# Where the block's closing barrier stands: behind the last projections or ahead of them

## The chip, the cores and the metric

The kernel runs on one core of one Trainium2 chip. The metric is the device time of one execution in microseconds (us), the slowest core's, which here is the only one. A profiled execution also has a *span*: the time from its first to its last recorded instruction. The device time is longer than the span by a time that no trace covers; that remainder is called "time minus span". All runs told of here are marked fast in the record.

In the profile's lines PE is TensorE, which multiplies matrices, DVE is VectorE, ACT ScalarE, POOL GpSimd and SP SyncE. The trace also records the clock that PE was granted: it is full (1.00) or half (0.50; in the trace of before 68 records of each), and it changes only on a grid of 3.413 us. A stretch between two points of this grid is called a *clock window* below, and how the grid lies against the kernel differs from execution to execution (it has a point at 1309.09 us in the profile of before). "Landing" is the moment when the data of a load has arrived.

## The reference, cut to what matters

Two one-token attention blocks whose results are concatenated. A has 32 heads over 32768 cached keys each, B has 32 query heads on 8 cached heads and looks at the last 4096 keys.

```python
def _A_ref(x, k_cache, v_cache, wq, wo):            # x 1x1x512, caches 1x32x32768x128, bf16
    q = (x @ wq).reshape(B, Sq, H, Dh).transpose(0, 2, 1, 3)
    scores = einsum("bhqd,bhkd->bhqk", q, k_cache) * Dh ** -0.5
    o = einsum("bhqk,bhkd->bhqd", softmax(scores), v_cache)
    return o.transpose(0, 2, 1, 3).reshape(B, Sq, H * Dh) @ wo     # wo 4096x512
# B: the same on k_cache[:, :, -4096:], each cached head repeated for 4 query heads
# result: concatenate([a, b], axis=-1), 1x1x1024
```

The caches that have to be read make 570 MB, so the kernel streams them and hides everything else behind the stream. Only its last 12 us concern us: the last head of A is finished (the products with V, called PV, and then the *gather*, two matmuls that collect the heads' results), spread over the partitions (the *spread*), and multiplied with `wo`; the row of B is multiplied with its `wo` there too.

## The kernel before

Every operation is recorded with its engine and its dependencies, and then each engine's list is emitted inside one block. At the end of the block all engines meet in a barrier. Behind it SyncE waits for the two stores of the output.

```python
def build(self):
    ...
    with nc.Block() as block:
        block.gpsimd(self.emit("pool"))
        block.vector(self.emit("dve"))
        block.scalar(self.emit("act"))
        block.sync(self.emit("sp"))
        block.tensor(self.emit("pe"))
    for n in self.X:                       # behind the closing barrier
        nc.sync.wait_ge(self.outsem[n], 16)

def emit(self, eng):
    ...                                    # what precedes the loop, the loop over the heads,
    def body(e):                           # and what follows it (post)
        ...
        with e.Fori(0, nit):
            ...
            for name, sem in sems.items():             # ends every pass of the loop: semaphores are set back
                e.sem_inc(sem, -step[name])._wait_ge(sem, step[name])
        ...
        straight(e, post, seen, base)

def plan(self):
    ...
    self.loop = {}
    for n in ("B", "A"):
        for part in range(len(self.WO_CUTS[n]) - 1):
            self.load_wo(n, part)          # wo of B in 2 pieces, wo of A in 6, each with its semaphore
    self.emit_spread("A")
    self.emit_proj()

def emit_spread(self, name):
    ...
    ri = self.op("dve", ... reciprocal(rinv, row sum) ..., self.gath)
    ob = self.op("dve", ... tensor_scalar_mul(ob, numerators, rinv) ..., ri)
    o = self.op("pe", mm, ob, self.k_sel)              # 4 matmuls: psT <- ob, spread
    t["ozop"] = self.op("dve", ... tensor_copy(oz, p2) ..., o)
```

`emit_proj` then has PE multiply B (32 matmuls into `psS`), lets VectorE copy the result to `pb`, sums it over the partitions (`psACC`), and multiplies A with the six pieces of its `wo` as they land (`psT`, then `psPT`). VectorE and ScalarE copy the two halves of the row to `out_sb`, and SyncE stores it.

Of the kernel before, what the change touches and what calls it, by code (L numbers as in the profile page):

```python
# [35 lines left out]
class Op:  # L36
# [2 lines left out]



    __slots__ = ("eng", "fn", "deps", "loop", "pos", "to", "users", "before", "alts")

    def __init__(self, eng, fn, deps, to, loop, alts=None):
        self.alts = alts
        self.eng = eng
        self.fn = fn
        self.deps = [d for d in deps if d is not None]
        self.to = to
        self.loop = loop  # L50
        self.users = []


class _Kernel:
# [31 lines left out]


    def op(self, eng, fn, *deps, to=None, alts=None):
        o = Op(eng, fn, deps, to, self.loop.get(eng), alts)
        self.prog[eng].append(o)  # L90
        return o

    def build(self):
        nc = self.nc
        self.alloc()
        self.plan()
        self.early(2)
        self.sems = {}
        for e in self.engines:
            self.assign(e)  # L100
        with nc.Block() as block:
            block.gpsimd(self.emit("pool"))
            block.vector(self.emit("dve"))
            block.scalar(self.emit("act"))
            block.sync(self.emit("sp"))
            block.tensor(self.emit("pe"))
        for n in self.X:
            nc.sync.wait_ge(self.outsem[n], 16)

# [63 lines left out]
        return need  # L173

    def emit(self, eng):
        ops = self.prog[eng]
        nit = len({o.loop for o in ops} - {None})
        its = [[o for o in ops if o.loop == k] for k in range(nit)]
        first = next((i for i, o in enumerate(ops) if o.loop is not None), len(ops))
        pre, post = ops[:first], ops[first + sum(map(len, its)):]  # L180

        def run(e, o, waits, fn=None):
            for sem, val in waits:
                e.wait_ge(sem, val)
            inst = (fn or o.fn)(e)
            if o.to:
                inst.then_inc(self.sem(eng, o.to), 1)

        def straight(e, part, seen, base):
            for o in part:  # L190
                waits = []
                for name, (sem, val) in self.needs(o).items():
                    if val > seen.get(name, 0):
                        seen[name] = val
                        waits.append((sem, val - base.get(name, 0)))
                run(e, o, waits)

        def body(e):
            seen, base = {}, {}
            straight(e, pre, seen, base)  # L200
            if not nit:
                return

            assert len(set(map(len, its))) == 1
            need = [[self.needs(o) for o in it] for it in its]
            top = lambda k, name: max(n[name][1] for n in need[k] if name in n)
            sems = {name: sem for it in need[-2:] for n in it for name, (sem, _) in n.items()}
            step = {name: top(-1, name) - top(-2, name) for name in sems}
            for name in [x for x in sems if not step[x]]:
                if top(0, name) > seen.get(name, 0):  # L210
                    e.wait_ge(sems[name], top(0, name))
                    seen[name] = top(0, name)
                del sems[name]
            start = {name: top(-2, name) - step[name] * (nit - 1) for name in sems}
            plans = []
            for k, it in enumerate(need):
                cur, plan = {}, []
                for n in it:
                    w = []
                    for name, (sem, val) in n.items():  # L220
                        if name not in sems:
                            continue
                        rel = val - start[name] - step[name] * k
                        if rel > cur.get(name, 0):
                            cur[name] = rel
                            w.append((name, rel))
                    plan.append(sorted(w))
                plans.append(plan)
            for k, plan in enumerate(plans):
                for p, q in zip(plan, plans[-1]):  # L230
                    assert p == q or (k == 0 and set(p) <= set(q)), (eng, k, p, q)
            for name, sem in sems.items():
                if start[name] > 0:
                    e.sem_inc(sem, -start[name])._wait_ge(sem, start[name])
                elif start[name] < 0:
                    e.sem_inc(sem, -start[name])
            groups = []
            for o, w in zip(its[-1], plans[-1]):
                if not (groups and groups[-1][0] and o.alts):
                    groups.append((bool(o.alts), []))  # L240
                groups[-1][1].append((o, [(sems[name], rel) for name, rel in w]))
            odd = None
            if any(two for two, _ in groups):
                assert nit % 2 == 0
                odd = e.alloc_register(f"{eng}_odd")
                e.reg_mov(odd, 0)
            with e.Fori(0, nit):
                for two, part in groups:
                    if two:
                        with e.If_eq(odd, 0):  # L250
                            for o, w in part:
                                run(e, o, w, o.alts[0])
                        with e.Else():
                            for o, w in part:
                                run(e, o, w, o.alts[1])
                    else:
                        for o, w in part:
                            run(e, o, w)
                if odd is not None:
                    e.reg_sub(odd, 1, odd)  # L260
                for name, sem in sems.items():
                    e.sem_inc(sem, -step[name])._wait_ge(sem, step[name])
            for name in sems:
                base[name] = seen[name] = start[name] + step[name] * nit
            straight(e, post, seen, base)

        return body
# [126 lines left out]
    def plan(self):  # L394
        self.lsem = {"k": self.ksem, "v": self.vsem}
        self.fill = {w: [0, 0] for w in "kv"}
        self.free = {"k": [None] * 3, "v": [None] * 2}
        self.nbatch = 0
        self.copies = []
        self.pending = []  # L400
        self.psread = self.ptread = self.sread = self.accread = None
        self.gath = self.qcopy = self.hcopy = self.qread = None
        self.constants()
        a, b = self.X["A"], self.X["B"]

        self.load_wq("B")
        self.load_b("k", 0)
        self.load_wq("A")
        self.load_b("k", 1)
        self.emit_qproj("B")  # L410
        self.emit_unit("B", 0)
        self.emit_qproj("A")
        self.emit_stats("B", 0)
        self.emit_unit("B", 1, {1: lambda: self.emit_PT("B", 0)})
        self.emit_stats("B", 1)
        for g in range(2):
            if g == 1:
                self.emit_PT("B", g)
            self.load_b("v", g)
            self.emit_PV("B", g)  # L420
        self.emit_spread("B")

        for g in range(NQH):
            self.loop = {"pe": g, "dve": g // 2}
            self.load_k(g, 1 if 0 < g < NQH - 1 else 2)
            self.load_v(g)
            self.emit_qcopy(g)
            self.emit_unit("A", g)
            self.emit_stats("A", g)
            self.emit_PT("A", g)  # L430
            self.emit_PV("A", g)
        self.loop = {}
        for n in ("B", "A"):
            for part in range(len(self.WO_CUTS[n]) - 1):
                self.load_wo(n, part)
        self.emit_spread("A")
        self.emit_proj()

# [344 lines left out]
```

## Time and profile before

| | before |
|---|---|
| device time | 1322.43 us, median of 6 runs (1322.35 to 1322.94) |
| the profiled execution | span 1321.7 us, device time 1323.36 us |
| DMA | busy 9 tenths in 39 of 40 slices, 432 GB/s |
| last V rows landed | 1299.2 us |
| last piece of `wo` of A landed | 1318.8 us |

The cache stream bounds the kernel as far as 1299 us. From there PE and VectorE work in turns, with `wo` still arriving. The timeline of before, its PE and VectorE lines from the last gather to the summing of B (start, duration, engine, line, operation; in brackets the idle time before it and what ended it):

```profile
1308.19 0.41 PE L683 MATMUL psG<-oc_A,hw 128*32 128x128 f32 x2 [1.64 <-DVE oc_A L672]
1308.63 0.15 DVE L693 RECIPROCAL rinv_A<-psG 32x1 f32<-32x1 f32 x1 [0.50 <-PE psG L683]
1308.82 0.34 DVE L694 TENSOR_SCALAR ob_A<-psG,rinv_A 32x128 bf16<-32x128 f32 x1
...
1309.40 0.28 PE L698 MATMUL psT<-ob_A,spread 32*128 32x32 bf16 x4 [0.81 <-DVE ob_A L694]
...
1309.61 3.31 PE L733 MATMUL psS<-kbuf,oz_B 128*1 128x512 bf16 x32
...
1312.97 0.69 DVE L736 COPY pb<-psS 128x512 f32<-128x512 f32 x1 [3.07 <-PE psS L733]
...
1313.71 1.02 PE L737 MATMUL psACC<-pb,e 128*1 128x512 f32 x2 [0.80 <-DVE pb L736]
```

VectorE starts its reciprocal after the end of the gather (L683; 1308.59), and has done both of its steps at 1309.16. PE could not have gone on earlier: its sequencer, whose records are branches and semaphore instructions, is ending the last pass of the loop until 1309.34. The two run side by side.

The pages of the profile leave out semaphore instructions, but the trace has them. These are its records of the end of before (start, duration, engine, what it waits for and signals; S97 and S96 are the barrier's, S113 and S114 the two stores'):

```
1320.545  0.248  Sync    DMA_DIRECT2D     out_dram<-out_sb
1320.851  0.206  Sync    DRAIN            $S[97]== $S[96]++
1321.082  0.017  GpSimd  EVENT_SEMAPHORE  $S[96]>= $S[96]-=
1321.161  0.017  GpSimd  EVENT_SEMAPHORE  $S[97]+=
1321.202  0.017  Sync    EVENT_SEMAPHORE  $S[97]>= $S[97]--
1321.286  0.373  Sync    EVENT_SEMAPHORE  $S[114]>= $S[113]>=
```

The store's completion reached S113 at 1321.636. So the barrier took place while the store was under way, and SyncE still had 0.37 us to wait.

### The profile page before, as it was taken

The page shows a single profiled execution, that of the slowest core. Times are in us where ns is not written, and L with a number is a line of the kernel's source. Part 1 is how long each engine was busy: PE and PEld are TensorE (multiplying, and loading weights), DVE is VectorE, ACT ScalarE, POOL GpSimd, SP SyncE. Part 2 cuts the span into 40 slices and gives each one's busy share as a digit, 9 for nine tenths or more (in the row PEclk, how much of TensorE's full clock was granted, in tenths as well). Part 3 has the DMA queues.
Part 4 walks back from the last instruction along what each step waited for, and adds up shares of the span by engine and source line. Part 5 has one row for each costly group of instructions (what it writes and reads, how often), then busy time and mean ns, then how long its engine had stood idle before and what let it go on. Part 6 is the DMA issues. An engine that isn't in the chain of part 4 may idle for free. (4 is left out here: it accounts for less than half of the span.)

```text
span 1321.7 us, 28783 instructions
## 1 busy us (share of the span) xinstructions
PE 968.2 (73%) x13243; PEld 673.7 (51%) x13243; DVE 750.7 (57%) x1341; ACT 55.1 (4%) x168; POOL 2.6 (0%) x22
## 2 busy tenths in 40 slices
PE   4675768777677878767787777678777667877787
PEld 3353446555444655544465544446554445555453
DVE  3563556664555666455566645556665456665563
ACT  0000000000000000000000000000000000000000
POOL 0000000000000000000000000000000000000000
PEclk9886788887878888787888878888887788888788
DMA  9999999999999999999999999999999999999998
GB/s 404 434 434 431 440 434 434 434 436 432 433 436 436 428 438 434 428 438 434 428 442 430 428 442 432 430 438 434 437 432 432 438 430 434 438 428 436 436 428 365
DMA packets 13359, 570.59 MB, mean 432 GB/s; under 512 B 1570, under 2 KB 1700, under 8 KB 2084
## 3 DMA queue, kind: packets, MB, share of 16 engines
q1 hardware_dynamic: 13060, 570.43, 99.8%
q8 instruction: 8, 0.13, 0.0%
q10 hardware_dynamic: 288, 0.00, 0.0%
q14 instruction: 3, 0.02, 0.0%
HBM read 570.43 MB, written 0.00 MB: 432 GB/s over the span
## 5 line engine op out<-in xcount | busy, mean ns | idle before, releaser
L557 DVE COPY kt<-psT 128x1024 bf16<-128x1024 bf16 x1056 | 654.3, 683 | 236.9 <-PE psT L553 235.5
L553 PE MATMUL psT<-ident,kbuf 128*128 128x128 bf16 x8448 | 577.8, 234 | 169.0 <-DMA kbuf<-in_A_k_cache_dram 154.4
L553 PEld LDWEIGHTS psT<-ident,kbuf 128*128 128x128 bf16 x8448 | 538.1, 106 | 261.2 <-DMA kbuf<-in_A_k_cache_dram 162.5
L656 PE MATMUL psACC<-vbuf,ptsb 128*4 128x512 bf16 (+1 forms) x2112 | 187.0, 531 | 22.8 <-ACT ptsb L631 22.0
L576 PE MATMUL psS<-kt,qw 128*32 128x512 bf16 x2048 | 157.7, 385 | 14.9 <-DVE kt L557 14.9
L670 DVE TENSOR_SCALAR oc_A<-psACC,hot_A 128x128 f32<-128x128 f32 x32 | 11.2, 350 | 251.9 <-PE psG L683 251.9
L656 PEld LDWEIGHTS psACC<-vbuf,ptsb 128*4 128x4 bf16 (+1 forms) x2112 | 59.8, 111 | 140.4 <-issue 93.1
L604 ACT ACTIVATE psb<-psS,nb_A 128x512 bf16<-128x512 f32 x32 | 22.0, 687 | 1166.5 <-DVE nb_A L603 1166.5
L576 PEld LDWEIGHTS psS<-kt,qw 128*32 128x32 bf16 x2048 | 34.0, 95 | 57.6 <-DVE kt L557 30.8
L683 PE MATMUL psG<-oc_A,hw 128*32 128x128 f32 (+1 forms) x128 | 19.3, 227 | 52.3 <-DVE oc_A L672 52.3
L683 PEld LDWEIGHTS psG<-oc_A,hw 128*32 128x32 f32 x128 | 11.4, 109 | 62.4 <-DVE oc_A L672 55.0
L628 PE MATMUL psPT<-ident,psb 128*128 128x128 bf16 x136 | 18.3, 279 | 34.0 <-ACT psb L604 34.0
L672 DVE SCALAR_TENSOR_TENSOR oc_A<-psACC,hot_A,oc_A 128x128 f32<-128x128 f32 x96 | 33.6, 350 | 3.4
L593 DVE TENSOR_REDUCE tr_in<-psS 128x1 f32<-128x512 f32 x34 | 23.5, 692 | 17.2 <-PE psS L576 17.2
L628 PEld LDWEIGHTS psPT<-ident,psb 128*128 128x128 bf16 x136 | 10.3, 119 | 37.1 <-ACT psb L604 36.7
L597 PE MATMUL psACC<-rows,tr_in 128*1 128x64 f32 x64 | 8.7, 217 | 25.6 <-DVE tr_in L593 25.6
L631 ACT ACTIVATE ptsb<-psPT 128x512 bf16<-128x512 bf16 x34 | 20.3, 597 | 30.9 <-PE psPT L628 30.9
L597 PEld LDWEIGHTS psACC<-rows,tr_in 128*1 128x1 f32 x64 | 2.7, 81 | 35.1 <-DVE tr_in L593 35.1
L601 PE MATMUL psACC<-mr_A,nscale 1*128 1x1 f32 x64 | 12.1, 256 | 9.8 <-DVE mr_A L600 9.8
L601 PEld LDWEIGHTS psACC<-mr_A,nscale 1*128 1x128 f32 x64 | 9.4, 182 | 15.8 <-DVE mr_A L600 15.8
L603 DVE COPY nb_A<-psACC 128x1 f32<-128x1 f32 x32 | 5.0, 157 | 15.1 <-PE psACC L601 15.1
L600 DVE TENSOR_REDUCE mr_A<-psACC 1x1 f32<-1x64 f32 x32 | 6.8, 213 | 11.7 <-PE psACC L597 11.7
(82 smaller groups left out, 74.9 us busy)
## 6 DMA issues: line engine op xcount, KB each, us to landing
kbuf<-in_A_k_cache_dram SPq DMA_DIRECT2D x4, 4096.0 KB, 23.2
kbuf<-in_B_k_cache_dram SPq DMA_DIRECT2D x2, 4096.0 KB, 31.6
vbuf<-in_B_v_cache_dram SPq DMA_DIRECT2D x2, 4096.0 KB, 25.4
vbuf<-in_B_wq_dram SPq DMA_DIRECT2D x1, 4096.0 KB, 12.4
vbuf<-in_A_wq_dram SPq DMA_DIRECT2D x1, 4096.0 KB, 31.9
kbuf<-in_B_wo_dram SPq DMA_DIRECT2D x2, 2048.0 KB, 33.1
kbuf<-in_A_wo_dram SPq DMA_DIRECT2D x1, 1408.0 KB, 27.4
kbuf<-in_A_wo_dram SPq DMA_DIRECT2D x1, 1024.0 KB, 29.5
```

The costliest lines, as they stand in the source:

```text
L553: inst = e.transpose(T[:, 128 * k:128 * k + 128], src[:, DH * k:DH * k + DH], self.ident[:, :])
L557: self.copies.append(self.op("dve", lambda v: v.tensor_copy(KT[:, :], T[:, :]), o, to="pe"))
L576: inst = e.matmul(self.S[32 * c:32 * c + 32, :], lhsT=win, rhs=self.kt[(bb + c // 2) % NKT][:, 512 * (c % 2):512 * (c % 2) + 512], start=b ...
L593: o = dve(lambda v: v.reduce_max(tr["in"][:, 0:1], self.S[:, :], axis=AXX), self.sdone, self.k_pool, to="pe" if name == "A" else None)
L597: o = self.op("pe", lambda e: e.matmul(self.ACC[0:1, 0:64], lhsT=tr["in"][:, 0:1], rhs=self.rows64[:, :], start=True, stop=True, skip_grou ...
L601: o = self.op("pe", lambda e: e.matmul(self.ACC[:, 64:65], lhsT=self.nscale[:, :], rhs=t["mr"][0:1, :], start=True, stop=True, skip_group_ ...
L604: self.sread = self.op("act", lambda s: s.activation(out=self.psb[:, :], in_=self.S[:, :], func=ACTF.Exp, bias=t["nb"][:, k:k + 1], scale= ...
L628: inst = e.transpose(PT[:, 128 * jj:128 * jj + 128], self.psb[:, 128 * jj:128 * jj + 128], self.ident[:, :])
L631: self.ptread = self.op("act", lambda s: s.activation(out=self.ptsb[:, :], in_=PT[:, 0:512], func=ACTF.Copy), self.psread, to="pe")
L656: inst = e.matmul(acc[32 * c:32 * c + rows, 0:512], lhsT=lhsT, rhs=rhs, start=begin, stop=end, tile_position=(0, 32 * c), skip_group_check ...
L672: o = self.op("dve", lambda v, src=src, hot=hot: v.scalar_tensor_tensor(out=oc, in0=src, scalar=hot, in1=oc, op0=ALU.mult, op1=ALU.add), p ...
L683: return self.op("pe", lambda e: e.matmul(self.G[0:32, c0 + c:c0 + c2], lhsT=win, rhs=t["oc"][g % len(t["oc"])][:, c:c2], start=False, sto ...
```

## The change

The intent: the barrier is taken from the end, where every engine has just finished and all wait for it, and put ahead of the spread and the projections. Each engine's operations that are recorded after the loads of `wo` form its tail, and the tails are emitted behind the block. SyncE's wait for the stores is then the last thing that happens.

```diff
+    # Op gets a field "tail"; op() fills it with self.tail, which plan() sets
         with nc.Block() as block:
             ...
             block.tensor(self.emit("pe"))
+        for eng, e in dict(pe=nc.tensor, dve=nc.vector, act=nc.scalar, sp=nc.sync).items():
+            self.rest[eng](e)
         for n in self.X:
             nc.sync.wait_ge(self.outsem[n], 16)
@@ emit
-        ops = self.prog[eng]
+        ops = [o for o in self.prog[eng] if not o.tail]
+        tail = [o for o in self.prog[eng] if o.tail]
@@ emit, body
             seen, base = {}, {}
+            self.rest[eng] = lambda e: straight(e, tail, seen, base)
@@ plan
                 self.load_wo(n, part)
+        self.tail = True
         self.emit_spread("A")
         self.emit_proj()
```

No operation is added or removed; both kernels have 28783 recorded instructions.

## The prediction

> **What bounds the kernel.** The page: span 1321.7 us, DMA busy 9 tenths in 39 of 40 slices. Until the last cache rows land (V of the last head at 1299.2 us, landings) the kernel waits for DMA. From there a serial chain of PE and DVE runs to the end (chain of waits), and the last wo pieces land at 1312.3, 1314.7, 1316.6, 1317.9, 1318.5 and 1318.8.

> **What it removes at the end: nothing that is waited for.** In the records of the last microseconds SyncE issues the last store 1320.55 to 1320.79, drains to 1321.06, is released by the barrier at 1321.20 and then waits from 1321.29 to 1321.66 for the store, whose completion lands at 1321.64. The barrier runs inside the store's own 0.84 us; after the change SyncE waits longer for the same landing. At most 0.3 us could appear outside the span, as four engines close earlier.

> **What it adds: a barrier in front of the tail.** In before, DVE runs reciprocal and scaling (1308.63 to 1309.16) while PE's sequencer leaves its loop (to 1309.34); PE starts L698 at 1309.40. After the change PE reaches the barrier last, at about 1309.4. Drain plus release costs about 0.25 us as in the opening barrier (last drain ends 1.05, engines released 1.20 to 1.26, next instruction about 1.28). Only then may DVE start its 0.53 us, and PE about 0.05 later: L698 at about 1310.25 to 1310.4. Estimate: 0.85 to 1.0 us later than before.

> **Prediction.** 1323.9 us, 1322.2 to 1325.8; within 2% nearly surely (0.99), 0.005 each for faster and slower by over 2%.

> **What would show it.** Timeline of the tail: L693 starts about 1 us later after L683 than before (0.02 us), PE idle between L683 and L698 about 1.7 us instead of 0.8; drains near 1309 instead of at the end; the last store issued later, its time to completion unchanged, SyncE's last wait about 0.8 us instead of 0.37; the clock in the last 12 us lower.

> **What would make it wrong.** If the closing sequence outside the span is bound by an engine other than SyncE, the time falls by 0.3 us or so. If the clock windows fall well, or the landings bind in most runs, it stays within 0.3 us. If the barrier costs more than in the opening, or the loop exit in front of it moves, it is up to 4 us slower.

## The result, and the profile after

The first measurement: 1322.58 us, median of six runs (1322.36 to 1323.42), against 1322.43 us before. The ratio is 1.0001, with a 95% interval from 0.9988 to 1.0014: the same. (A ratio is the mean time of one kernel's fast runs over that of the other's of the same rounds, so not quite the ratio of the quoted medians.) Five further runs of the same kernel gave 1322.58, 1322.62, 1324.12, 1326.65 and 1326.77 us; the spread is the main matter below.

The timeline of the first profile of after (lines are numbered 7 higher):

```profile
1307.14 0.41 PE L690 MATMUL psG<-oc_A,hw 128*32 128x128 f32 x2 [1.63 <-DVE oc_A L679]
1308.64 0.16 DVE L700 RECIPROCAL rinv_A<-psG 32x1 f32<-32x1 f32 x1 [1.55 <-PEq L102]
1308.84 0.34 DVE L701 TENSOR_SCALAR ob_A<-psG,rinv_A 32x128 bf16<-32x128 f32 x1
...
1309.23 0.26 PE L705 MATMUL psT<-ob_A,spread 32*128 32x32 bf16 x4 [1.68 <-DVE ob_A L701]
...
1309.42 1.90 PE L740 MATMUL psS<-kbuf,oz_B 128*1 128x512 bf16 x32
...
1312.12 1.02 PE L744 MATMUL psACC<-pb,e 128*1 128x512 f32 x2 [0.80 <-DVE pb L743]
```

The reciprocal is now held by "PEq L102", which is PE's arrival at the barrier, and starts 1.09 us after the end of the gather instead of 0.04. The records show the barrier itself:

```
1308.196  0.076  Tensor  COMPARE_BRANCH   (the loop's last instruction)
1308.360  0.008  Tensor  DRAIN            $S[97]== $S[96]++
1308.405  0.017  GpSimd  EVENT_SEMAPHORE  $S[96]>= $S[96]-=
1308.483  0.017  GpSimd  EVENT_SEMAPHORE  $S[97]+=
1308.536  0.021  Vector  EVENT_SEMAPHORE  $S[97]>= $S[97]--
...
1319.741  0.249  Sync    DMA_DIRECT2D     out_dram<-out_sb
1320.036  0.821  Sync    EVENT_SEMAPHORE  $S[114]>= $S[113]>=
```

Count from the gather to PE's next matmul, for the gather itself came earlier here for other reasons (the matmuls ahead of it, PV, started 0.33 us earlier and ran at full clock from 1303.92 on: 5.60 us instead of 6.30). From the end of the gather to the spread it is 1309.40 − 1308.59 = 0.81 us before, and 1309.23 − 1307.55 = 1.68 us after. The move cost PE 0.87 us. At the other end it gained nothing: from the last store's issue to SyncE's last instruction it is 1.11 us before and 1.12 us after, the wait having grown from 0.37 to 0.82 us.

Yet the span is 0.8 us shorter in this profile. Its chain of waits says why (start, duration, what):

```profile
1285.21 31.52 DMA kbuf<-in_A_wo_dram
1316.73 0.04 issue
1316.78 2.45 PE psPT L726 x29
1319.22 0.02 issue
1319.25 0.41 DVE out_sb L733
```

PE waited for `wo` here. The last piece landed at 1318.90, and 1.96 us later the kernel was over, whatever had happened before. (Three other profiles, with no closing barrier, end 1.96 or 1.97 us after their last landing, too; that landing came at 1318.70 to 1318.99.) In the profile of before PE was late by itself, as its chain shows:

```profile
1309.40 0.28 PE psT L698 x4
1309.67 3.27 PE psS L733 x32
1312.95 0.02 issue
1312.97 0.70 DVE pb L736
1313.67 0.04 issue
1313.71 1.02 PE psACC L737 x2
1314.73 2.27 PE psT L741 x11
1317.01 3.02 PE psPT L719 x42
```

There the end came 2.84 us after the last landing. So the two profiles differ mostly in the clock that PE was granted (from 1309.09 to 1312.50 it is 0.50 in before, whose L733 takes 3.31 us; in after it is 1.00 from 1303.92 on, and the same 32 matmuls, L740, take 1.90 us), and not by the change. A comparison has to be of executions whose clock windows fell alike, or else of many.

### The profile page after: what moved, and what is told of

It reads as the page before. It is cut to its first block, busy times and chain, and to the rows that moved or that the text cites. A ratio compares the mean times of both kernels' runs of the same rounds, so it can differ in the third digit from the quotient of the medians.

```text
span 1320.9 us, 28783 instructions
## 1 busy us (share of the span) xinstructions
PE 968.6 (73%) x13243; PEld 676.8 (51%) x13243; DVE 752.6 (57%) x1341; ACT 55.2 (4%) x168; POOL 2.6 (0%) x22
## 5 line engine op out<-in xcount | busy, mean ns | idle before, releaser
L663 PE MATMUL psACC<-vbuf,ptsb 128*4 128x512 bf16 (+1 forms) x2112 | 183.9, 524 | 22.8 <-ACT ptsb L638 22.0
L502 PE MATMUL psACC<-vbuf,x_B 128*2 128x512 bf16 x32 | 3.5, 616 | 13.8 <-DMA x_B<-in_B_x_dram 13.8
```

Of the source, the lines that this page charges most:

```text
L663: inst = e.matmul(acc[32 * c:32 * c + rows, 0:512], lhsT=lhsT, rhs=rhs, start=begin, stop=end, tile_position=(0, 32 * c), skip_group_check ...
```

## The experiments

Three questions. Was the closing barrier free? What does the barrier cost in its new place, and what absorbs it? And what is in the time that no trace covers? The theory at the start: the closing barrier was hidden in the store's completion; the new place costs PE about 0.9 us; the landings absorb it when PE's clock is full, and when it is not, the cost goes through or grows. The rival: both places cost about the same, and cancel.

### Group one: the barrier taken out, doubled, and moved by two operations

These four ran on one chip, with nine runs of before at 1323.02 us median (1322.41 to 1323.48).

**No closing barrier at all** (from before):

```diff
             block.tensor(self.emit("pe"))
+        end = nc.main_func.blocks[-1]
+        assert end.name.endswith("_end") and len(end.instructions) == 11
+        end.instructions = []
         for n in self.X:
```

> Before with its closing barrier taken out and put nowhere. Theory (the closing barrier was hidden in the last store's completion, and the tail is bound by the landings of the last wo pieces): within 0.2 us of before, median 1322.3 to 1322.6; SyncE's last wait grows from 0.37 to about 0.8 us, the last store's completion about 0.84 us after its issue ends. Rival (taking the closing barrier from the end saves its 0.3 to 0.4 us, and the barrier in front of the tail gives them back): 1322.0 to 1322.1, 0.3 us or more faster than before and than after.

Measured: 1322.17 us (1321.93 to 1323.15), ratio 0.9996, interval 0.9982 to 1.001. SyncE's last wait was 0.82 us, and from the store's issue to the end it took 1.12 us: inside the span the barrier had cost nothing, as the theory has it. The mean span was 1321.06 us against 1321.26 for before's nine. But the median is 0.85 us lower, against the expectation (the rival's 1322.0 to 1322.1 is nearer), and 0.46 us of that sits outside the span: time minus span was 1.23 to 1.29 us in all five runs, and 1.68 to 1.75 in all nine of before. Neither theory had said this. Group three takes it up.

**Both barriers** (from after):

```diff
             self.rest[eng](e)
+        nc.all_engine_barrier()
         for n in self.X:
```

> After, with a second barrier put back at the end in front of SyncE's last wait. Theory: as after within 0.2 us (1322.4 to 1322.7); SyncE's last wait back at about 0.37 us. Rival (a closing barrier costs 0.3 to 0.4 us): 1322.9 or more.

Measured: 1323.12 us (1322.19 to 1324.43). The median is the rival's number. But the five runs scatter as those of after do (spans from 1320.9 to 1323.1 us), so it decides nothing; the profile does: from the store's issue to the end 1.12 us, the last wait 0.38 us. Adding a closing barrier lengthened nothing inside the span. Time minus span was 1.31 us, *less* than the 1.62 of after, with one barrier more.

**After, once more:**

> After, unchanged, for more draws of the clock windows. Theory (landings bind in nearly all runs): median 1322.5, no run beyond 1323.5. My prediction's model (six runs in ten 1.3 to 3.4 us slower): most runs above 1323.7.

Measured: 1324.12 us (1322.58 to 1326.77). Two of the five runs are 4 us slower than the two fastest, and the theory's "no run beyond 1323.5" fell. The expectation from my model, most runs above 1323.7, holds for this set (three of five) and not for the first (none of six). The profiled run was one of the slow ones, and by luck its clock windows lie within 0.2 us of those in the profile of before, which makes it the pair that was wanted. The windows of before, cut where the clock may change (the stretch, its length, each engine's busy time with its instruction count, then PE's clock, DMA share and GB/s):

```profile
1305.68:1309.09 3.41, 1.28 (x20) 0.54 (x12) 1.83 (x6) 0.00 (x0) 0.00 (x0) 1.00 0.99 421
1309.09:1312.50 3.41, 3.10 (x32) 1.11 (x36) 0.26 (x2) 0.00 (x0) 0.00 (x0) 0.50 0.98 415
1312.50:1315.92 3.42, 2.62 (x17) 0.72 (x10) 1.37 (x2) 0.00 (x0) 0.00 (x0) 1.00 1.01 420
1315.92:1319.33 3.41, 3.41 (x44) 1.74 (x44) 0.68 (x1) 0.00 (x0) 0.00 (x0) 1.00 0.51 199
```

and those of this run of after:

```profile
1305.83:1309.24 3.41, 1.28 (x20) 0.55 (x12) 1.40 (x4) 0.00 (x0) 0.00 (x0) 1.00 0.96 411
1309.24:1312.66 3.42, 2.23 (x24) 0.83 (x28) 0.69 (x3) 0.00 (x0) 0.00 (x0) 0.50 1.02 432
1312.66:1316.07 3.41, 2.61 (x18) 0.49 (x11) 0.69 (x1) 0.00 (x0) 0.00 (x0) 0.50 0.98 408
1316.07:1319.48 3.41, 3.41 (x8) 0.90 (x7) 0.68 (x1) 0.00 (x0) 0.00 (x0) 0.50 0.53 204
```

The first window is the same in both, PE busy 1.28 us, and both are at half clock (0.50) after it. In the second, PE of before is busy for 3.10 of 3.41 us (0.91), and the window after it is at 1.00. In after PE starts later and is busy for 2.23 us (0.65, as the prediction had estimated), and the window after it is at 0.50. The third window is busy for 0.77 of its length and is followed by 0.50 too; the fourth, busy throughout, is followed by 1.00. The chain of waits of this run shows what PE lost:

```profile
1310.43 0.28 PE psT L705 x4
1310.71 3.54 PE psS L740 x32
...
1315.02 1.87 PE psACC L744 x2
1316.89 3.62 PE psT L748 x11
1320.50 3.03 PE psPT L726 x42
```

Against before: the spread starts 1.03 us later (0.87 by the move, 0.16 because the gather ended later), L740 takes 0.27 us longer, L744 0.85 and L748 1.35, the rest 0.01. That sums to 3.51 us, and the spans are 1321.66 and 1325.17 us. From the last landing (1319.12) to the end it is 6.05 us, so the landings no longer hide anything.

**The two VectorE steps ahead of the barrier** (from after):

```diff
-        self.tail = True
         self.emit_spread("A")
@@ emit_spread
         ob = self.op("dve", ... tensor_scalar_mul ...)
+        self.tail = name == "A"
         def mm(e):
```

> After, with the reciprocal and the scaling on VectorE emitted ahead of the barrier, so that only PE's spread and what follows stand behind it. Theory: the barrier's 0.91 us on PE is about 0.3 us of drain and release plus 0.6 us of VectorE work that had run beside PE's loop exit; so PE starts the spread about 0.3 us after the branch of its loop ends, not 0.95, and the total stays within 0.2 us of after because the landings bind. Rival (the 0.91 us is all barrier): PE starts it about 0.9 us after the branch here too.

Measured: 1323.30 us (1322.58 to 1324.03). Its timeline:

```profile
1309.40 0.41 PE L689 MATMUL psG<-oc_A,hw 128*32 128x128 f32 x2 [1.64 <-DVE oc_A L678]
1309.85 0.16 DVE L699 RECIPROCAL rinv_A<-psG 32x1 f32<-32x1 f32 x1 [0.50 <-PE psG L689]
1310.04 0.34 DVE L700 TENSOR_SCALAR ob_A<-psG,rinv_A 32x128 bf16<-32x128 f32 x1
1310.87 0.25 PE L705 MATMUL psT<-ob_A,spread 32*128 32x32 bf16 x4 [1.06 <-PEq L102]
```

The reciprocal follows the gather again, and the spread is released by the barrier itself. It starts 0.34 us after the end of the loop's branch; in after it is 0.96 and 0.93, in before 0.06. So of the 0.9 us about 0.3 is the barrier, and 0.6 is VectorE work that had run beside the loop's exit and now stands behind it. The rival fell. The time did not follow "within 0.2 us of after": it is 0.7 above the first set of after and 0.8 under the second, inside their scatter.

### Group two: without the landings

If the landings absorb the cost, taking them away should show it. The six loads of `wo` of A are left out, and PE multiplies with what the cache left in that buffer. PE's work is the same, and half of the output is wrong. The edit, applied to four kernels:

```diff
-        for n in ("B", "A"):
-            for part in range(len(self.WO_CUTS[n]) - 1):
-                self.load_wo(n, part)
+        for part in range(len(self.WO_CUTS["B"]) - 1):
+            self.load_wo("B", part)
@@ proj_part; the last matmuls of emit_proj likewise
-        deps = (self.wosem[name][part], 16), self.c[name]["ozop"]
+        deps = (self.wosem[name][part], 16) if name == "B" else None, self.c[name]["ozop"]
```

The four expectations, and then the four results; before, in the same rounds, had 1322.74 us (1322.44 to 1323.26).

Before without the loads:

> Before without the six loads of wo of A: PE reads what the cache left in that buffer (half of the output is wrong on purpose), so no landing after 1309 us can hold the tail. Theory: the chain of PE alone decides; 0.3 to 2 us faster than before, with more spread, for the clock windows now show. This is the base of the next three.

After without the loads:

> After without those loads. Theory (the barrier's 0.91 us sits on PE's chain and the landings absorbed it): at least 0.7 us slower than before without the loads, 0.9 us where the clock windows fall alike, up to 3.9 us where half clock stays longer. Rival (the barrier costs nothing on PE's chain, or removing the closing one pays for it): within 0.3 us of it.

No closing barrier, without the loads:

> No barrier at all after the opening one, without those loads. Theory (the closing barrier is hidden in the store's completion, which has nothing to do with the loads): as before without the loads within 0.2 us. Rival (the closing barrier costs its 0.3 us): 0.3 us faster than it.

The VectorE steps ahead of the barrier, without the loads:

> After with the two VectorE steps ahead of the barrier, without those loads. Theory: about 0.3 us slower than before without the loads where the clock windows fall alike, so about 0.6 us faster than after without the loads. Rival (all of the 0.91 us is the barrier itself): as after without the loads.

| without the loads | time, median (range), us | the five spans, us | gather to spread, us | time minus span, us |
|---|---|---|---|---|
| before | 1322.62 (1321.89 to 1323.37) | 1320.2, 1320.2, 1320.9, 1321.6, 1321.7 | 0.81 | 1.69 |
| after | 1323.81 (1322.22 to 1327.13) | 1320.6, 1321.0, 1322.2, 1322.3, 1325.5 | 1.65 | 1.61 |
| no closing barrier | 1320.78 (1320.38 to 1323.06) | 1319.1, 1319.5, 1319.5, 1321.3, 1321.8 | 0.78 | 1.26 |
| VectorE steps first | 1323.38 (1321.39 to 1323.43) | 1319.7, 1321.7, 1321.7, 1321.8, 1321.8 | 1.09 | 1.64 |

("Gather to spread" and the records behind it are from each kernel's profile.) What this settles: with no landing to wait for, the spans go below the 1320.7 us that no run of before with its loads went under (27 runs with a span: 1320.7 to 1321.8). So those 1320.7 us are the landings' bound. And the barrier's cost is on PE's chain: 0.84 us from gather to spread. The times agree, with after 1.4 us longer than before in the mean of the spans (1322.3 against 1320.9). By themselves they would not settle it: with five runs of each the difference of the mean times is 1.3 us with a standard error of 0.9, so the rival's "within 0.3 us" falls by the records and not by the times. The third expectation missed: without the closing barrier the mean span is 0.7 us below that of before without the loads, instead of within 0.2. The profiles of the two have the same tail (from the start of PV to the end 21.41 and 21.47 us, both with a half-clock window in the middle), so I read it as the draw of the clock windows, which five runs don't average out; that reading is argued, not shown. The fourth is not settled by its times for the same reason; its profile repeats 0.34 us from the branch to the spread.

### Group three: the end, and the time outside the span

Nine runs of before in these rounds: 1322.79 us (1322.38 to 1323.39).

**No closing barrier, again:**

> The kernel with no closing barrier again, for more draws. Theory (inside the span the closing barrier was hidden; outside the span, the time minus the span was 1.26 us in all its runs against 1.72 of before): median 0.3 to 0.7 us under before of the same rounds, time minus span 1.26 again. Rival (the earlier 1322.17 was a lucky draw of the clock windows): within 0.2 us of before.

Measured: 1322.11 us (1321.86 to 1323.32), 0.68 us under before; ratio 0.9995, interval 0.9982 to 1.0009. Time minus span 1.24 us, before 1.70. The mean span is 1321.04 against 1321.18 us. So the 0.46 us outside repeats.

**Before, with a second barrier behind the opening one:**

```diff
             self.assign(e)
+        nc.all_engine_barrier()
         with nc.Block() as block:
```

> Before with a second barrier right behind the opening one, where every engine waits for loads anyway; its end is untouched. Rival one (the time minus the span depends on how many instructions stand in the streams, not on the closing barrier: the kernel with both barriers had 1.31): time minus span falls to about 1.3 and the time by 0.4 us. Rival two (it depends on what the engines do at the end): time minus span stays 1.72, and the time within 0.2 us of before.

Measured: 1322.32 us (1322.11 to 1322.93); time minus span 1.33 us. A barrier *more* at the start, where PE waits for a load anyway (until 13.31 us in the profile of before), took 0.4 us off, with the end unchanged (the last wait is 0.38 us).

**No closing barrier, and a second one behind the opening one** (both edits):

> No closing barrier, but a second one right behind the opening one: as many instructions in each stream as before. Rival one (number of instructions): time minus span back at about 1.7. Rival two (what the engines do at the end): 1.26, as without the second opening barrier.

Measured: 1323.05 us (1322.34 to 1323.47); time minus span 1.60 us. The gain is gone, with the end still free of a barrier. Of the two rivals the first fits: the time outside the span follows how many barriers stand in the program. Whether it is the number of barriers or of instructions these runs can't tell, as each barrier brings the same instructions.

**Before, with three more barriers at the end:**

```diff
             block.tensor(self.emit("pe"))
+        for _ in range(3):
+            nc.all_engine_barrier()
         for n in self.X:
```

> Before with three more barriers at its end, ahead of SyncE's last wait. Theory (the first barrier is hidden in the 1.11 us from the last store's issue to its completion, with 0.37 us to spare): the last wait shrinks to nothing and from the store's issue to the end it takes 1.5 to 2.0 us, so 0.4 to 0.9 us slower than before. Rival (closing barriers are not hidden, each costs 0.25 to 0.4 us): from the store's issue to the end 1.9 to 2.3 us.

Measured: 1323.90 us (1323.45 to 1324.82). SyncE's records:

```
1319.866  0.249  DMA_DIRECT2D     out_dram<-out_sb
1320.525  0.017  EVENT_SEMAPHORE  $S[97]>= $S[97]--      (first barrier)
1320.858  0.017  EVENT_SEMAPHORE  $S[97]>= $S[97]--
1321.185  0.017  EVENT_SEMAPHORE  $S[97]>= $S[97]--
1321.513  0.017  EVENT_SEMAPHORE  $S[97]>= $S[97]--
1321.584  0.028  EVENT_SEMAPHORE  $S[114]>= $S[113]>=
```

Each further barrier takes 0.33 us, the store's completion (1320.96) comes while they run, and the last wait is down to 0.03 us. From the store's issue to the end it is 1.75 us instead of 1.11: three times 0.33 less the 0.35 us to spare is 0.64. The first barrier is hidden and the further ones are not, as the theory said; the rival had asked for 1.9 or more. The total rose by more than the 0.4 to 0.9 us expected: the median is 1.11 us above before's, 0.68 us of it in the mean span and 0.42 us in the time outside, which the expectation had not reckoned with.

Time minus span, over all kernels (means of five to six runs each; before, over 27 runs, 1.71):

| barriers, with the opening one | kernels | time minus span, us |
|---|---|---|
| 1 | no closing barrier, three sets | 1.24 to 1.26 |
| 2 | before; after and its variants; none at the end but two at the start | 1.60 to 1.71 |
| 3 | both barriers; before with two at the start | 1.31, 1.33 |
| 5 | before with three more at the end | 2.12 |

It goes by the number of barriers, up and down, and it is the same with and without the six loads, so the six instructions fewer in SyncE's stream don't move it. Within the row of two there is a smaller step: the kernels whose second barrier stands at the end have 1.71 and 1.69 us (before, with and without the loads), those in which it stands elsewhere 1.60 to 1.64. More than that the traces don't show, as none of them covers this time. Its cause stays open.

## Why the prediction was right or wrong

The time, 1322.58 us, lies inside the predicted range and within 2%. The point, 1323.9, was 1.3 us too high for the first six runs. By step:

- *The end gains nothing that is waited for.* Right. From the store's issue to the end: 1.11 us before, 1.12 after, 1.12 with both barriers, 1.12 with none; and the barrier becomes visible only when there are more (group three). In before the store was issued at 1320.55, its packets had ended at 1321.31, and its completion came at 1321.64, so 0.33 of the 1.09 us lies behind its last packet.
- *The new place costs PE 0.85 to 1.0 us.* Right: 0.87, 0.87 and 0.87 us in three profiles with the barrier there and the loads in place, and 0.3 of it is barrier (the fourth experiment).
- *Drains near 1309, last wait about 0.8 us, reciprocal 1 us after the gather.* Right: 1308.4, 0.82, 1.09. Two other signs failed in the first profile and came only in the slow one: a later last store (1319.74 against 1320.55 before; 1324.05 in the slow one), and a lower clock (from 1303.92 on no half-clock window before the last store, where before has one at 1309.09; three in the slow one).
- *Where the windows fall badly, half clock stays one or two windows more.* Right in kind, and shown by the pair: two windows more, 3.51 us, a little above the 1.3 to 3.4 that I gave.
- *About four phases in ten cost nothing, the mean is about 1.8 us.* This is the term that was mis-sized. Of eleven runs of after, seven have a span of at most 1321.1 us, which is the landings' bound with its small scatter; one more is within before's range; three are beyond it (1322.5, 1325.0, 1325.2). The mean span of the eleven is 1321.9 us against 1321.2 for 27 runs of before: 0.7 us, not 1.8. (The prediction doesn't say whether its mean is over all phases or over the costly six in ten; if over these alone, it comes to about 1.1 us over all.) The step that failed is the rule I took from the trace, "a full one by half if busy under 0.5". That limit is too high: in the trace of before, four of the eight full-clock windows that were busy for 0.475 to 0.5 kept full clock, and in all fourteen traces together 45 of 69. In the tail it matters. Two profiles with the barrier in the new place (both barriers; after without the loads) have a window there that was busy for 0.48 and 0.49 and was followed by full clock, and the first profile of after has two at 0.52 and 0.51 (their lines in this order, columns as before):

```profile
1306.75:1310.16 3.41, 1.65 (x28) 0.69 (x20) 1.40 (x4) 0.00 (x0) 0.00 (x0) 1.00 0.97 413
...
1306.35:1309.77 3.42, 1.69 (x28) 0.73 (x20) 1.40 (x4) 0.00 (x0) 0.00 (x0) 1.00 0.34 144
...
1303.92:1307.33 3.41, 1.78 (x32) 0.82 (x24) 1.40 (x4) 0.00 (x0) 0.00 (x0) 1.00 0.98 420
1307.33:1310.75 3.42, 1.74 (x34) 0.77 (x36) 0.69 (x3) 0.00 (x0) 0.00 (x0) 1.00 1.01 428
```

By the rule the first two would have fallen to half clock, and they did not. That this made my model count too many slow phases is argued and not shown, for the model was not run again with a lower limit. The draw may have helped as well: if six phases in ten were costly and each run drew its phase anew, at most four costly runs of eleven would still come up about one time in ten. So how much of the difference is the rule and how much is luck stays open.

- *At most 0.3 us outside the span, because engines close earlier.* The size holds: 1.71 to 1.62. The reason was my guess and is not shown, for no trace covers this time. Among the kernels with two barriers those without one at the end do have about 0.1 us less, which fits it; but the larger moves of this time in group three, up and down by 0.4 us, came from a barrier at the start, with the end untouched.

So the change removes a barrier that nobody waited for, and puts one where PE waits. The landings of `wo` hide it in most executions. In the others it costs more, up to about 4 us; in the one pair of executions whose clock windows fell alike it is 3.51 us.

The kernel with no closing barrier had the lowest medians with correct results, 1322.17 and 1322.11 us, against 1323.02 and 1322.79 of before in the same rounds. That is 0.7 to 0.9 us, more than half of it outside the span. The intervals of both ratios include 1, and as the gain goes by the number of barriers for a cause that is not known, it isn't one to build on.

## What to carry to other kernels

Before a barrier, or any other closing step, is moved, look in the trace at what runs beside it: behind the issue of this kernel's last store there is 1.11 us in which one barrier is free, while ahead of the tail it also puts in sequence what had run side by side (0.6 of the 0.9 us here). In the pair of executions whose windows fell alike, a delay of 1.03 us became 3.51 us: PE's busy share of one window went from 0.91 to 0.65, and half clock stayed two windows longer. Other executions of the same kernel kept full clock (the first profile of after, from 1303.92 us on). So read the windows of busy time, and compare executions whose windows fell alike, or many. A bound that hides a cost, here the last landing, hides it only as long as PE comes in time: from that landing to the end it took 1.96 us where PE had waited for it, and 2.84 and 6.05 us where PE came later.

## What else the traces show

- How busy PE was in the windows before its clock changed. In the trace of before, of 57 half-clock windows in which PE was busy less than 0.775 of the time none was followed by full clock, and of 70 above that 67 were. Of the full-clock windows (without the four of the first clock record and the last one, which reaches beyond the span), all 62 under 0.475 were followed by half clock and all 177 above 0.525 were not; of the nine between them four were. These counts give no sharp limit: of two windows there at 0.479, the one from 1145.25 us was followed by half clock and the one from 1271.55 us by full clock.
- SyncE's last instruction, which waits for two semaphores, has a record that grows with its wait: 0.03 us (before with three more barriers), 0.37 (before) and 0.82 (after), as the store's completion came earlier or later against it.
- The time of a barrier of all engines inside this kernel: 0.33 us from one to the next in a row (before with three more at the end), and from the end of the last engine's drain to the release 0.15 us at the end of before and 0.17 us in after.
